# Block 0 of a convolution and GELU-MLP kernel in two column halves, with W_in in four parts, W_out right behind it, and the early x loads moved to the hardware DMA ring

## The chip, the cores and the metric

One core of a Trainium2 chip. The metric is device time of one execution in microseconds (us); smaller is better. Single executions of the kernel before agree within about 0.3% (685.96 to 687.88 us in the rounds of the experiments). The experiments ran on four chips; the kernel before ran in each round, and each time is held against it.

Names used below: PE is TensorE (matmul), PEld its weight load, DVE is VectorE, ACT ScalarE, POOL GpSimd, SP SyncE. DMA transfers issued by GpSimd go through the software ring (its queue moved 2.56 MB in the profile before, which is the sum of what GpSimd issued), those issued by SyncE and ScalarE through hardware rings (their queues moved 48.78 and 0.59 MB, again the sums of what each issued). A *block* is a stretch of tokens, 256 wide for blocks 0 to 5 and 512 wide after that, taken twice: once in each half of the tokens. A *third* is one of three groups of channels of a block's convolution. A *slice* is one of the pieces of the first multiply of a block, each ended by one GELU of 1024 columns.

## The reference

```python
def _attn_ref(x, weight):                  # x (8, 4096, 192), weight (8, 7)
    w = np.exp(weight - np.max(weight, axis=-1, keepdims=True))
    w = w / (np.sum(w, axis=-1, keepdims=True) + 1e-09)
    # causal convolution over the sequence, 7 taps, one set of taps per head of 24 channels
    ...
    out = np.einsum('hk,bskhg->bshg', w, x_unf)

def _moe_ref(x, w_in, w_out):              # x (32768, 192), w_in (192, 2048), w_out (2048, 192)
    h = x @ w_in
    g = 0.5 * h * (1.0 + erf(h * inv_sqrt2))
    return (g @ w_out).astype(np.float32)
```

Convolution, first multiply, exact GELU, second multiply. All tensors are float32; the kernel multiplies in bf16.

## The kernel before

For blocks 0 and 1 the convolution runs on PE, as multiplies with diagonal weights, 7 taps for each third and each of two row halves. From block 2 on it runs on VectorE, as a chain of fused multiply-adds. So VectorE must keep ahead of PE from then on, while it also takes the finished convolution of block 1 out of PSUM. The orders, cut out and put side by side:

```python
WS = [256] * 6 + [512] * ((HALF - 1536) // 512)
PC = {0: 0, 1: 1}                       # blocks convolved on PE
SW = {1: (2, 3), 2: (0, 2, 1, 3), 3: (0, 2, 1, 3)}   # x loads in the software ring
CONVB = {0: [0, 1, 2], 1: [3, 0, 1]}    # PSUM banks of the thirds
FP = [0, FQ, 2 * FQ, FH]                # W_in in three parts: 1/4, 1/4, 1/2 of a half

# GpSimd: order of its loads
for i in range(3):
    win_in(FP[i], FP[i + 1], S_WIN[i])
...
halo(0)
load(g, 1, SW[1], S_XG[1])
load(g, 2, SW[2], S_XG[2])
g.dma_start(<W_out>).then_inc(S_WOUT, 16)
halo(1)
load(g, 3, SW[3], S_XG[3])

# VectorE: order at the head
diag(0); diag(1)                        # diagonal weights
for p in range(NP): trans(0, p)         # 32x32 transposes of x
diag(2)
dup(0); dup(1); dup(2)                  # second copy of W_in for the other row half
for p in range(NP): trans(1, p)
for p in range(NP): cast(1, p)
# from here the list of block 2: transposes (op 0 to 2), then the convolution;
# evictions of block 1's thirds stand ahead of op 0, 3 and 5
side = [((2, (0, 3, 5)[p]), conv_out, 1, p) for p in range(NP)]

# PE: first multiply of block 0, with thirds of block 1 behind slices 4, 5, 6
for p in range(NP):
    behind[0, 4 + p] = [(1, p, k) for k in range(KS - 1, -1, -1)]

# SyncE
load(sp, 0, (0, 1))
sp.wait_ge(S_WIN[0], 32)
load(sp, 1, (0, 1))
sp.wait_ge(S_XG[3], 64)
for n in range(1, NB):
    if n + 3 < NB:
        load(sp, n + 3)
    ...
```

The order on VectorE: the eviction of block 1's first third, then three transposes of block 2's x, then the other two evictions.

## Time and profile before

| | before |
|---|---|
| time, median of 3 (range) | 686.16 us (686.04 to 686.56) |
| span of the profiled execution | 684.5 us |
| PE busy | 677.3 us (99%) |
| x of block 2 | software ring, ahead of W_out; VectorE doesn't wait for it |
| W_out | 768 KB, issue to landing 8.6 us |
| first second-multiply of block 0's values (taken together with block 1's first multiplies) | 21.11 us |

The last row is the *marker* of this document. From there PE is busy almost without a gap (55.43 of 55.50 us in the stretch that the prediction shows), so a shift of the marker should be a shift of the end. The times of landings and waits are of the profiled execution.

### The profile page before, as it was taken

How to read it: one execution, taken by the hardware profiler on the slowest of the kernel's cores; microseconds unless marked ns; L12 is line 12 of the kernel's file. 1: busy time of each engine (PE TensorE's matmuls, PEld its weight loads, DVE VectorE, ACT ScalarE, POOL GpSimd, SP SyncE). 2: the span in 40 equal slices, each digit the busy share in tenths (PEclk: the TensorE clock that was granted, in tenths of full speed). 3: DMA queues.
4: the chain of work that ended last, by engine and by line, in shares of the span. 5: the costliest groups of instructions: out<-in, count | busy, mean ns of one | idle time of the engine just before them, and what ended most of it. 6: DMA issues, size and time to landing. Idle time of an engine off the chain costs nothing.

```text
span 684.5 us, 27314 instructions
## 1 busy us (share of the span) xinstructions
PE 677.3 (99%) x12548; PEld 409.0 (60%) x12548; DVE 580.5 (85%) x914; ACT 532.6 (78%) x536; POOL 46.0 (7%) x97
## 2 busy tenths in 40 slices
PE   8999999999999999999999999999999999999997
PEld 4899655555555555555555555555555555555556
DVE  7999999888899888898888898888898888998702
ACT  6788987877787777787877878777778777877771
POOL 8110000000000000000000000000000000000000
PEclk9999999999999999999999999999999999999999
DMA  8544531344432344422444422444322444221224
GB/s 135 95 107 99 117 61 32 64 94 95 94 67 50 76 94 95 93 52 55 85 94 95 88 51 53 95 94 95 72 54 66 95 94 95 61 53 31 48 49 94
DMA packets 133234, 53.66 MB, mean 78 GB/s; under 512 B 127552, under 2 KB 132960, under 8 KB 133120
## 3 DMA queue, kind: packets, MB, share of 16 engines
q1 hardware_dynamic: 128144, 48.78, 33.3%
q0 software_dynamic: 3792, 2.56, 2.4%
q8 instruction: 98, 1.61, 1.0%
q10 hardware_dynamic: 1184, 0.59, 0.3%
q14 instruction: 16, 0.13, 0.1%
HBM read 28.31 MB, written 25.17 MB: 78 GB/s over the span
## 4 chain that ended last, share of the span: by engine, by line
PE 96%; ACT 2%; DMA 1%; issue 0%; DVE 0%; SPq 0%
PE hp L683 47%; PE ob L747 42%; PE ob L714 6%; ACT gT L612 2%; PE ob L640 1%; DMA xin<-in_x_dram 1%; ACT osb L227 0%; DVE osb L247 0%; SPq L258 0%; DVE osb L229 0%; DVE xT L478 0%; ACT xTb L572 0%; SPq L795 0%; ACT xc L579 0%
## 5 line engine op out<-in xcount | busy, mean ns | idle before, releaser
L612 ACT ACTIVATE gT<-hp 128x1024 bf16<-128x1024 f32 x512 | 523.4, 1024 | 132.7 <-PE hp L683 129.6
L683 PE MATMUL hp<-xc,win 64*64 64x512 bf16 (+2 forms) x6048 | 418.5, 366 | 1.1 <-ACT gT L612 0.7
L747 PE MATMUL ob<-gT,wout 64*64 64x512 bf16 x5376 | 366.3, 376 | 0.0
L508 DVE SCALAR_TENSOR_TENSOR acc<-xT,wcol,acc 128x512 f32<-128x512 f32 (+1 forms) x495 | 314.0, 697 | 0.0
L683 PEld LDWEIGHTS hp<-xc,win 64*64 64x64 bf16 (+1 forms) x6048 | 187.7, 106 | 135.6 <-ACT gT L612 2.1
L747 PEld LDWEIGHTS ob<-gT,wout 64*64 64x64 bf16 x5376 | 172.1, 118 | 123.0
L247 DVE STREAM_TRANSPOSE osb<-ob 128x512 f32<-128x512 f32 x84 | 73.7, 880 | 86.8 <-PE ob L747 86.8
L478 DVE STREAM_TRANSPOSE xT<-xin 128x512 f32<-128x512 f32 (+1 forms) x105 | 78.5, 799 | 0.2 <-DMA xin<-in_x_dram 0.2
L508 DVE SCALAR_TENSOR_TENSOR xc<-xT,wcol,acc 128x512 bf16<-128x512 f32 (+1 forms) x99 | 65.1, 711 | 0.0
L374 POOL COPY xT<-xT 128x558 f32<-128x558 f32 x33 | 21.6, 654 | 578.6 <-DVE xT L478 578.6
L501 DVE TENSOR_SCALAR acc<-xT,wcol 128x512 f32<-128x512 f32 (+1 forms) x99 | 56.1, 618 | 1.1
L714 PE MATMUL ob<-wout,gT 64*128 64x192 bf16 x1024 | 52.2, 243 | 0.3
L714 PEld LDWEIGHTS ob<-wout,gT 64*128 64x128 bf16 x1024 | 43.5, 94 | 6.5 <-PE ob L714 0.6
L357 POOL COPY xT<-xT 128x18 f32<-128x18 f32 x30 | 11.6, 387 | 1.4 <-DVE xc L461 1.4
L229 DVE COPY osb<-ob 128x384 f32<-128x384 f32 x4 | 2.2, 557 | 7.8 <-PE ob L714 7.8
L625 PE MATMUL hp<-warm 128*128 128x512 bf16 x16 | 5.7, 533 | 1.3 <-DVE warm L394 1.3
L640 PE MATMUL ob<-xTb,dg 64*64 64x256 bf16 x84 | 5.3, 271 | 1.1 <-ACT xTb L572 1.1
L227 ACT ACTIVATE osb<-ob 128x384 f32<-128x384 f32 x12 | 5.8, 486 | 0.0
L258 POOL DMA_DIRECT2D xin<-in_x_dram x10 | 5.8, 588 | 0.0
L640 PEld LDWEIGHTS ob<-xTb,dg 64*64 64x64 bf16 x84 | 4.3, 106 | 2.2 <-ACT xTb L572 1.6
L625 PEld LDWEIGHTS hp<-warm 128*128 128x128 bf16 x16 | 2.0, 129 | 4.5 <-issue 2.7
L324 POOL DMA_DIRECT2D win<-in_moe_w_in_dram x6 | 3.9, 651 | 0.0
(32 smaller groups left out, 21.7 us busy)
## 6 DMA issues: line engine op xcount, KB each, us to landing
xin<-in_x_dram SPq DMA_DIRECT2D x116, 192.0 KB, 4.4
out_dram<-osb SPq DMA_DIRECT2D x112, 192.0 KB, 3.6
out_dram<-osb SPq DMA_DIRECT2D x56, 48.0 KB, 1.7
xin<-in_x_dram SPq DMA_DIRECT2D x12, 96.0 KB, 2.7
xin<-in_x_dram POOLq DMA_DIRECT2D x10, 96.0 KB, 2.7
wout<-in_moe_w_out_dram POOLq DMA_DIRECT2D x1, 768.0 KB, 8.6
win<-in_moe_w_in_dram POOLq DMA_DIRECT2D x4, 96.0 KB, 4.2
win<-in_moe_w_in_dram POOLq DMA_DIRECT2D x2, 192.0 KB, 5.3
```

Source lines behind the costliest of these rows:

```text
L247: v.transpose(ap(osb[m % 2], j, [[8 * C, 128], [C // 2, TB // 32], [NP, 32]]), bank(ring(m, j)),).then_inc(S_EV)
L357: g.tensor_copy(dst, ap(xT[(n - 1) % 2], WS[n - 1] + 31, [[NP * XW, 128], [XW, NP], [32, HB]],),).then_inc(S_HALO)
L374: g.tensor_copy(ap(t, 1, [[NP * tw, 128], [tw, NP], [32, HB], [1, 31]]), ap(t, WS[n], [[NP * tw, 128], [tw, NP], [32, HB], [1, 31]]),).the ...
L478: v.transpose(ap(xT[n % 2], p * XW + HL, [[NP * XW, 128], [1, w]]), ap(xin[n % NX], p, [[TB // 32 * DQ, 128], [DQ, w // 32], [NP, 32]],),) ...
L501: ins = v.tensor_scalar(a, src, wk, None, ALU.mult)
L508: ins = v.scalar_tensor_tensor(dst, src, wk, a, op0=ALU.mult, op1=ALU.add)
L612: a.activation(out=ap(gT[n % 2], i * c * 2 * w, dst), in_=ap(hp[u % 2], 0, src), func=AF.Gelu,).then_inc(S_GELU)
L625: t.matmul(hp[1][:, 0:512], warm[:, 0:128], warm[:, :])
L640: ins = t.matmul(bank(CONVB[n][p], r, w), dg[r, d0 : d0 + 64], xTb[PC[n]][r, x0 : x0 + w], start=(k == KS - 1), stop=(k == 0), tile_positi ...
L683: ins = t.matmul(hp[u % 2][fo : fo + fw, o : o + w], win[r, f1 : f1 + fw], xc[n % 2][r, p * TB : p * TB + w], start=(p == 0), stop=(p == N ...
L714: ins = t.matmul(bank(bb[sub], w=C), gT[m % 2][r, c0 : c0 + 128], wout[r, CH[i] * C : (CH[i] + 1) * C], start=(ph == 0 and i == 0), stop=( ...
L747: ins = t.matmul(bank(ring(m, j), slice(64 * h, 64 * h + 64), w), ap(wout, 64 * hf * NF * C + CH[i] * C + j, [[NF * C, 64], [NP, 64]],), g ...
```

## The change

Its intent: block 0 is split into two halves of 128 columns, so that PE can begin the first multiply after half the convolution. W_in comes in four equal parts, so that slices wait for less. W_out follows it at once in the software ring. The x of blocks 1, 2 and 3 moves to SyncE's hardware ring, behind waits for W_in's fourth part (block 2) and for W_out (block 3); half of block 1's was there before. The x of block 0 is loaded as long rows, and ScalarE makes a third of the diagonal weights. Cut to its core:

```diff
+    PARTS = [(0, 0, 128, (0, 1, 2)), (0, 128, 128, (3, 0, 1)), (1, 0, 256, (2, 3, 0))]
-        SW = {1: (2, 3), 2: (0, 2, 1, 3), 3: (0, 2, 1, 3)}
-        FP = [0, FQ, 2 * FQ, FH]
+        FP = [0, FQ, 2 * FQ, 3 * FQ, FH]
 ... # load(): block 0 as one long row for each partition
+                if n == 0:
+                    dst = [[TB // 32 * DQ, 32], [1, mb * D - DQ]]
+                    src = [[mb * D, 32], [1, mb * D - DQ]]
 ... # GpSimd; the loop ahead of it still loads parts 0 to 2
             halo(0)
-            load(g, 1, SW[1], S_XG[1])
-            load(g, 2, SW[2], S_XG[2])
+            win_in(FP[3], FP[4], S_WIN[3])
             g.dma_start(<W_out>)
             halo(1)
-            load(g, 3, SW[3], S_XG[3])
 ... # VectorE
             diag(0)
+            trans(0, 0)
             diag(1)
-            for p in range(NP):
-                trans(0, p)
-            diag(2)
+            trans(0, 1)
+            trans(0, 2)
             dup(0)
             dup(1)
+            for p in range(NP):
+                cast(1, p)
             dup(2)
+            conv_out(1, 0)
+            dup(3)
+            conv_out(1, 1)
+            conv_out(1, 2)
             for p in range(NP):
                 trans(1, p)
             for p in range(NP):
-                cast(1, p)
+                cast(2, p)
 ... # ScalarE: third set of diagonal weights, casts and evictions of the first half
+            for k in range(KS):
+                a.activation(<64 columns of dg>, func=AF.Copy, scale=<one tap>)
+            cast0(0)
+            cast0(1)
+            conv_out0(0)
+            cast0(2)
+            conv_out0(1)
+            conv_out0(2)
 ... # PE: slices 0 to 3 are the first half, 4 to 7 the second, each 24 matmuls of 128 columns
-                behind[0, 4 + p] = [(1, p, k) for k in range(KS - 1, -1, -1)]
+            behind = {
+                1: third(1, 0),
+                2: third(1, 1) + third(1, 2),
+                4: third(2, 0),
+                5: third(2, 1),
+                6: third(2, 2),
+            }
 ... # SyncE
             sp.wait_ge(S_WIN[0], 32)
-            load(sp, 1, (0, 1))
-            sp.wait_ge(S_XG[3], 64)
+            load(sp, 1)
+            sp.wait_ge(S_WIN[3], 32)
+            load(sp, 2)
+            sp.wait_ge(S_WOUT, 16)
+            load(sp, 3)
```

More of the change, by code (lines that the diff above doesn't have):

```diff
@@ L128, in bass_lightweight_conv__then__act_gelu_exact_kernel @@
         ob = pst("ob", [128, 2048])
-        SW = {1: (2, 3), 2: (0, 2, 1, 3), 3: (0, 2, 1, 3)}
         S_WSB = sem("S_WSB")
-        S_WIN = [sem("S_WIN%d" % i) for i in range(3)]
+        S_WIN = [sem("S_WIN%d" % i) for i in range(4)]
         S_WOUT = sem("S_WOUT")
-        S_XG = {n: sem("S_XG%d" % n) for n in SW}
         S_XIN = [sem("S_XIN%d" % i) for i in range(NX)]
@@ L145, in bass_lightweight_conv__then__act_gelu_exact_kernel @@
         S_HOT = sem("S_HOT")
-        S_CAST = [sem("S_CAST%d" % i) for i in range(len(PC))]
+        S_CAST = [sem("S_CAST%d" % i) for i in range(len(PARTS))]
+        S_DGA = sem("S_DGA")
         S_PC = sem("S_PC")
@@ L163, in bank @@
             return ob[r, 512 * (b % 4) : 512 * (b % 4) + w]
-        CONVB = {0: [0, 1, 2], 1: [3, 0, 1]}
         NCV = NP * KS
@@ L170, in bass_lightweight_conv__then__act_gelu_exact_kernel, with pce @@
         FH = F // 2
-        FP = [0, FQ, 2 * FQ, FH]
+        FP = [0, FQ, 2 * FQ, 3 * FQ, FH]
         def cvd(n):
             return NCV * sum(m not in PC for m in range(n + 1))
-        def pce(n, p):
-            return NP * PC[n] + p + 1
+        def pce(i, p):
+            return NP * i + p + 1
         HC = [0]
@@ L190, in xin_at @@
         def xin_at(n):
-            return sum(64 - 16 * len(SW.get(m, ())) for m in range(n % NX, n + 1, NX))
+            return 64 * (n // NX + 1)
         def banks(m, g):
@@ L257, in load @@
                 off = ((q // 2) * HALF + OFF[n]) * D + DQ * (q % 2)
-                e.dma_start(
-                    ap(
-                        xin[n % NX],
-                        32 * q * (TB // 32 * DQ),
-                        [[TB // 32 * DQ, 32], [DQ, mb], [1, DQ]],
-                    ),
-                    ap(xt, off, [[mb * D, 32], [D, mb], [1, DQ]]),
+                dst = [[TB // 32 * DQ, 32], [DQ, mb], [1, DQ]]
+                src = [[mb * D, 32], [D, mb], [1, DQ]]
+                if n == 0:
+                    dst = [[TB // 32 * DQ, 32], [1, mb * D - DQ]]
+                    src = [[mb * D, 32], [1, mb * D - DQ]]
+                e.dma_start(
+                    ap(xin[n % NX], 32 * q * (TB // 32 * DQ), dst), ap(xt, off, src)
                 ).then_inc(sm or S_XIN[n % NX], 16)
@@ L349, in halo @@
                     if n - 2 in PC:
-                        g.wait_ge(S_PCE, pce(n - 2, NP - 1))
+                        g.wait_ge(S_PCE, pce(n - 1, NP - 1))
                     else:
@@ L450, in dup, with cast, conv_out @@
                     ).then_inc(S_DUPE)
-            def cast(n, p):
+            def cast(i, p):
+                n, c0, w, _ = PARTS[i]
                 v.wait_ge(S_TR, NP * n + p + 1)
                 v.tensor_copy(
-                    ap(xTb[PC[n]], p * XB + HL, [[NP * XB, 128], [1, WS[n]]]),
-                    ap(xT[n % 2], p * XW + HL, [[NP * XW, 128], [1, WS[n]]]),
-                ).then_inc(S_CAST[PC[n]])
-            def conv_out(n, p):
-                v.wait_ge(S_PC, pce(n, p))
+                    ap(xTb[PC[n]], p * XB + HL + c0, [[NP * XB, 128], [1, w]]),
+                    ap(xT[n % 2], p * XW + HL + c0, [[NP * XW, 128], [1, w]]),
+                ).then_inc(S_CAST[i])
+            def conv_out(i, p):
+                n, c0, w, bk = PARTS[i]
+                v.wait_ge(S_PC, pce(i, p))
                 v.tensor_copy(
-                    xc[n % 2][:, p * TB : p * TB + WS[n]], bank(CONVB[n][p], w=WS[n])
+                    xc[n % 2][:, p * TB + c0 : p * TB + c0 + w], bank(bk[p], w=w)
                 ).then_inc(S_PCE)
@@ L469, in trans @@
                         v.wait_ge(S_XIN[n % NX], xin_at(n))
-                    if n in SW:
-                        v.wait_ge(S_XG[n], 16 * len(SW[n]))
                     if n >= 2 and n - 2 in PC:
-                        v.wait_ge(S_PCE, pce(n - 2, NP - 1))
+                        v.wait_ge(S_PCE, pce(n - 1, NP - 1))
                     elif n >= 2:
@@ L482, in trans @@
                         p,
-                        [[TB // 32 * DQ, 128], [DQ, w // 32], [NP, 32]],
+                        [[TB // 32 * DQ, 128], [D if n == 0 else DQ, w // 32], [NP, 32]],
                     ),
@@ L533, in _ @@
             for p in range(NP):
-                cast(1, p)
-            side = [((2, (0, 3, 5)[p]), conv_out, 1, p) for p in range(NP)]
+                cast(2, p)
+            side = [((2, (0, 3, 5)[p]), conv_out, 2, p) for p in range(NP)]
             for n in range(M0, M1):
@@ L569, in _, with cast0, conv_out0 @@
             a.activation(out=hot[:, 1:2], in_=warm[0:1, 0:1], func=AF.Gelu).then_inc(S_HOT)
-            for p in range(NP):
+            a.wait_ge(S_PRO, 10)
+            a.wait_ge(S_IDN, 2)
+            for k in range(KS):
+                d0 = ((NP - 1) * KS + k) * 64
+                c0 = (NP - 1) * 32 + k
+                a.activation(
+                    out=dg[:, d0 : d0 + 64],
+                    in_=idb[:, :],
+                    func=AF.Copy,
+                    scale=wcol[:, c0 : c0 + 1],
+                ).then_inc(S_DGA)
+            _, _, w0, bk0 = PARTS[0]
+            def cast0(p):
                 a.wait_ge(S_TR, p + 1)
                 a.activation(
-                    out=ap(xTb[0], p * XB + HL, [[NP * XB, 128], [1, WS[0]]]),
-                    in_=ap(xT[0], p * XW + HL, [[NP * XW, 128], [1, WS[0]]]),
+                    out=ap(xTb[0], p * XB + HL, [[NP * XB, 128], [1, w0]]),
+                    in_=ap(xT[0], p * XW + HL, [[NP * XW, 128], [1, w0]]),
                     func=AF.Copy,
                 ).then_inc(S_CAST[0])
-            for p in range(NP):
+            def conv_out0(p):
                 a.wait_ge(S_PC, p + 1)
                 a.activation(
-                    out=xc[0][:, p * TB : p * TB + WS[0]],
-                    in_=bank(CONVB[0][p], w=WS[0]),
-                    func=AF.Copy,
+                    out=xc[0][:, p * TB : p * TB + w0], in_=bank(bk0[p], w=w0), func=AF.Copy
                 ).then_inc(S_PCE)
+            cast0(0)
[4 more added lines that the diff above has]
+            conv_out0(2)
             due = {(1, 6): [(0, 0)]}
@@ L599, in _ @@
                         a.wait_ge(S_MM2, MMC[n - 1])
-                    if M0 <= n < M1:
+                    g0 = i * c * 2 * w
+                    if n == 0:
+                        src = [[2 * TB, 128], [TB, 2], [128, 4], [1, 128]]
+                        dst = [[NF * 2 * TB, 128], [128, 2], [512, 4], [1, 128]]
+                        g0 = i % 4 * 4 * 512 + i // 4 * 256
+                    elif M0 <= n < M1:
                         src = [[2 * TB, 128], [1, 2 * TB]]
@@ L612, in _ @@
                     a.activation(
-                        out=ap(gT[n % 2], i * c * 2 * w, dst),
+                        out=ap(gT[n % 2], g0, dst),
                         in_=ap(hp[u % 2], 0, src),
@@ L625, in _, with pconv @@
                 t.matmul(hp[1][:, 0:512], warm[:, 0:128], warm[:, :])
-            def pconv(n, p, k):
-                w = WS[n]
+            def pconv(i, p, k):
+                n, c0, w, bk = PARTS[i]
                 if k == KS - 1:
-                    t.wait_ge(S_CAST[PC[n]], p + 1)
-                    if n == 0:
-                        t.wait_ge(S_DG, p + 1)
-                if k == KS - 2:
+                    t.wait_ge(S_CAST[i], p + 1)
+                    if i == 0:
+                        if p < NP - 1:
+                            t.wait_ge(S_DG, p + 1)
+                        else:
+                            t.wait_ge(S_DGA, KS)
+                if k == KS - 2 and c0 == 0:
                     t.wait_ge(S_HALO, HC[n] + 2 + p)
@@ L638, in pconv @@
                     d0 = (p * KS + k) * 64
-                    x0 = p * XB + 32 * k
+                    x0 = p * XB + 32 * k + c0
                     ins = t.matmul(
-                        bank(CONVB[n][p], r, w),
+                        bank(bk[p], r, w),
                         dg[r, d0 : d0 + 64],
@@ L649, in pconv, with third @@
                     ins.then_inc(S_PC)
-            taps = [(p, k) for p in range(NP) for k in range(KS - 1, -1, -1)]
-            for p, k in taps:
-                pconv(0, p, k)
-            behind = {}
+            def third(i, p):
+                return [(i, p, k) for k in range(KS - 1, -1, -1)]
             for p in range(NP):
-                behind[0, 4 + p] = [(1, p, k) for k in range(KS - 1, -1, -1)]
+                for q in third(0, p):
+                    pconv(*q)
+            behind = {
[5 more added lines that the diff above has]
+            }
             def mm1(n, i):
@@ L663, in mm1 @@
                     t.wait_ge(S_GELU, u - 1)
-                if i == 0:
-                    if n in PC:
-                        t.wait_ge(S_PCE, pce(n, NP - 2))
-                    else:
-                        t.wait_ge(S_CV, cvd(n))
-                if n == 0 and i in (0, 2, 4):
-                    t.wait_ge(S_WIN[i // 2], 32)
-                    t.wait_ge(S_DUPE, 2 * (i // 2) + 2)
+                part = {(0, 0): 0, (0, 4): 1, (1, 0): 2}.get((n, i))
+                if part is not None:
+                    t.wait_ge(S_PCE, pce(part, NP - 2))
+                elif i == 0:
+                    t.wait_ge(S_CV, cvd(n))
+                x0 = 0
+                if n == 0:
+                    w, c = 128, 4
+                    x0 = i // 4 * w
+                    if i < 4:
+                        t.wait_ge(S_WIN[i], 32)
+                        t.wait_ge(S_DUPE, 2 * i + 2)
                 for cc in range(c):
-                    f0 = 128 * CH[i * c + cc]
+                    f0 = 128 * CH[(i * c + cc) % NF]
                     for p in range(NP):
-                        if n in PC and i == 0 and cc == 0 and p == NP - 1:
-                            t.wait_ge(S_PCE, pce(n, p))
+                        if part is not None and cc == 0 and p == NP - 1:
+                            t.wait_ge(S_PCE, pce(part, p))
                         for hf in range(2):
@@ L685, in mm1 @@
                                     win[r, f1 : f1 + fw],
-                                    xc[n % 2][r, p * TB : p * TB + w],
+                                    xc[n % 2][r, p * TB + x0 : p * TB + x0 + w],
                                     start=(p == 0),
@@ L702, in mm2 @@
                         t.wait_ge(S_PH, PHC[m] + g + 1)
-                if g == 0 and ph == 0:
+                if m == 0:
+                    if ph == 0 and i == 0:
+                        t.wait_ge(S_GELU, 4 * g + 4)
+                elif g == 0 and ph == 0:
                     c = NCH[m]
@@ L775, in _ @@
                     mm1(n, i)
-                    for q in behind.get((n, i), []):
+                    for q in behind.get(i, []) if n == 0 else []:
                         pconv(*q)
```

## The prediction

> **What bounds the kernel now.** I read the page first: the matrix engine (PE) is busy 677.3 of 684.5 us and PE lines hold 96% of the chain that ended last. So only the start, the joins between stages and the end can give anything. Since the change edits the first two blocks only, I then read the chain of waits of the first 60 us.
>
> ```profile
> 2.04 4.96 DMA xin<-in_x_dram
> ...
> 7.03 0.53 DVE xT L478
> ...
> 7.58 0.43 ACT xTb L572
> ...
> 8.04 2.50 PE ob L640 x42
> ...
> 11.01 0.63 PE hp L683 x8
> ...
> 11.66 1.94 ACT gT L612 x2
> ...
> 13.61 1.03 ACT gT L612
> ...
> 14.69 0.83 PE hp L683 x12
> 15.51 0.88 PE ob L640 x14
> 16.40 0.76 PE hp L683 x12
> 17.16 0.88 PE ob L640 x14
> 18.04 0.76 PE hp L683 x12
> 18.80 0.88 PE ob L640 x14
> 19.68 1.42 PE hp L683 x24
> ```
>
> Columns: start, length, what. The head is serial to 11.0: x lands (7.0), transpose, cast, block 0's convolution on PE, eviction. Then three GELUs pace PE to 14.7. From 14.69 there is nothing but PE: four first multiplies and three thirds of block 1's convolution in turn, and the last entry is slice 7 of block 0 with slice 0 of block 1, so block 1 begins at about 20.35 (19.68 and half of 1.42, less the tail). All that this change can win lies before that moment; whatever it adds to PE after the first multiply is paid in full unless it fills PE's idle time.
>
> From the table of stretches: PE has no room after that.
>
> ```profile
> 24.50:80.00 55.50, 55.43 (x1134) 49.95 (x1132) 55.33 (x115) 46.79 (x54) 4.62 (x10) 1.00 0.46 100
> ```
>
> PE is busy 55.43 of 55.50 us, but VectorE (third pair, 55.33) is full too, so I looked in the timeline at where the two meet most closely, block 6, the first of width 512:
>
> ```profile
> 70.81 2.07 DVE L508 SCALAR_TENSOR_TENSOR xc<-xT,wcol,acc 128x512 bf16<-128x512 f32 x3
> ...
> 73.55 0.81 PE L683 MATMUL hp<-xc,win 64*128 64x512 bf16 x6
> ```
>
> VectorE ends block 6's convolution at 72.88, PE needs it at about 73.5: only 0.6 us of slack. A gain in PE's start reaches the end only if VectorE's run of convolutions moves with it.
>
> [...] twelve 256-wide matmuls (six pairs on two row halves) take 0.66 us, 110 ns a pair[...]; sixteen 192-wide ones 0.66, 82 a pair[...]. [...] In this trace loads of 64x128 last 92 to 96 ns and those of 64x64 102 to 107; the smaller is the slower[...]. The convolution's weights are 64x64. [...] x moves as 384-byte packets, 22 to 35 ns each in this trace's head, some 11 to 17 bytes per ns. [...] Trace: 256 elements in 384 to 417 ns, 1024 in 1024[...].
>
> **Part by part.**
>
> *Load of x, block 0.* Rows of 5760 B in place of 15 pieces of 384 B, twice the bytes (0.74 MB in all against 0.39). [...] I put the landing at 5.3 to 5.9, against 7.0. But VectorE's chain for the convolution weights ends at 5.64 and the first diagonal build (0.58) now comes first: transpose (0,0) runs 6.26 to 6.78, against 7.56 before, and (0,1), (0,2) end at 7.85 and 8.29, since the second build stands between. The last transpose before ended at 8.35: nothing gained there.
>
> *ScalarE.* Seven scaled copies of 64 columns replace VectorE's third build (0.58): about 0.3 us each, 0.25 apart, so 5.7 to 7.6. They hold back the first cast from 6.8 to 7.6. Casts and evictions of 128 are 107 ns shorter (0.31 and 0.28). In order: cast 0 to 7.9, cast 1 to 8.3, eviction 0 at 8.6 to 9.0, cast 2 to 9.3, eviction 1 to 9.6, eviction 2 at about 10.4. PE's third third waits for cast 2. The multiply's last operand is ready at 10.4 against 10.96: 0.55 us won.
>
> *Convolution, PE.* 42 matmuls more (84 of 128 wide and 42 of 256 instead of 84 of 256). At 256 wide a third takes 0.77 to 0.88. At 128 wide it is 7 pairs of 56 ns if the stream decides, 0.4; about 100 ns a pair if the 64x64 weight load does (107 seen, less a little overlap), 0.7. The new three thirds are thus 1.2 to 2.1 us more on PE.
>
> *First multiply, block 0.* Eight slices of 24 matmuls of 128 columns instead of 12 of 256. Stream-bound: 12 x 56 = 0.67 us a slice, as now. [...]
>
> *W_in and copies.* The last part is issued after block 0's halo, at about 8.75, and by the 2.4 to 4.2 us that loads in this ring take lands near 12.3. VectorE: copies of parts 0 and 1 (0.45 to 0.5 each half) to 10.1, casts of the second half to 10.8, part 2 to 11.8, then eviction (1,0), part 3, the other two evictions, three transposes (1.34), casts of block 1.
>
> *Weights out, early x.* W_out lands earlier (some 18 against 21.1), but the 0.29 us that the weight load waited for it leaves no gap on PE. x of blocks 2 and 3 comes later but before VectorE wants it. Nothing on the path.
>
> **The two sums.** *Stream-bound:* first multiply from 10.1; slice 2 ends at 12.6; slice 3 waits for part 3's copy (12.3 + 0.9), 13.2 to 13.9; slice 4 to 14.5; the convolution of block 1 waits for VectorE: 13.75, transposes to 15.1, cast to 15.5; then 3 x 0.77 + 3 x 0.68 = 4.4, block 1 begins at 19.9: 0.45 us earlier. [...] The difference passes whole to the end: VectorE's last eviction of block 1 follows the same third of the convolution, so its run of convolutions shifts with PE and the 0.6 us of slack stays.
>
> **Rivals.** *A gain by filling the idle PE:* between 8.04 and 14.69 PE does 5.1 us of work in 6.65, so 1.5 us is idle; with the head's 0.55 this would make 684.2 if nothing were added. [...] *x lands late:* twice the bytes against W_in in the same 16 engines, which are full from 5 us; if it lands at 7.5, everything moves 0.7 to 1.2 us later: about 688.5. For: the DMA share is near its top there. Against: fifteen times fewer pieces. *VectorE or part 3 of W_in becomes the bound:* part 3 late by 1 us adds up to 1 us in the stream-bound case[...]. *Hidden anyway:* block 6 waits for VectorE, and a gain over 0.6 us is lost there; caps the good case near 685.5.
>
> **Range and chances.** I give the two sums even weight: -0.45 and +2.15, mean +0.9 on 686.16: 687.1. The lower end takes the stream-bound sum with 0.5 us more luck, the upper the load-bound one with 0.6 us of bad luck. 2% is 13.7 us, more than the whole head but for a few us, so within 2% is all but sure.
>
> **What would show it.** [...] Thirds of the convolution at 128: 0.4 or 0.7. The transpose at 6.26 behind the diagonal build, not behind the load. First multiply's wait for the eviction over at 10.4. Start of block 1: 19.9 or 22.5, and every later block shifted by the same. I'm wrong if block 1 starts before 19.3, if a later block's wait eats or adds a shift, or if the time after the head changes.

The forecast of 687.1 us is the mean of two sums for the start of block 1. The stream-bound sum came to 19.9 us, 0.45 earlier than before. The load-bound sum came to about 22.5 us, 2.15 later. The trace before has no matmul 128 columns wide. The 56 ns a pair is what the changed kernel then showed (24 more matmuls took 0.67 us). The 100 ns a pair is an estimate from the 107 ns of the 64x64 weight loads. On ScalarE of the changed kernel the seven scaled copies took 333 ns each, 0.24 us apart, and casts and evictions of 128 columns 302 and 277 ns, against 417 and 384 for 256 columns before.

## More of the kernel before

VectorE's timeline before, around the x of block 2. The columns are start, length, engine, line, operation, output and inputs, count, and in brackets the idle time ahead of it with what ended it.

```profile
16.44 0.42 DVE L461 CAST xc<-ob 128x256 bf16<-128x256 f32 x1 [1.61 <-PE ob L640]
16.78 1.33 DVE L478 STREAM_TRANSPOSE xT<-xin 128x256 f32<-128x256 f32 x3
18.08 0.42 DVE L461 CAST xc<-ob 128x256 bf16<-128x256 f32 x1
```

The first line is the eviction of block 1's first third, the second the transposes of block 2, the third the second eviction. There is no bracket at the transposes: x was there.

## The result, and the profile after

| | before | after |
|---|---|---|
| time, median (range), 4 runs each, same chip | 686.36 us (686.04 to 686.72) | 689.88 us (689.59 to 690.09) |
| ratio after / before, 95% interval | | 1.0051 (1.0033 to 1.0068) |
| span of the profiled execution | 684.5 us | 688.2 us |
| marker | 21.11 us | 24.40 us |
| start of VectorE's last eviction | 681.08 us | 684.35 us |

Ratios are the mean time of one kernel's fast runs over that of the other's fast runs of the same rounds, so they are not quite the ratio of the medians quoted here. The change makes the kernel 3.5 us slower: within 2%, but outside the predicted range of 685.2 to 688.9.

The last two rows say where: the marker is 3.29 us later and the last eviction 3.27 us. Of the span's 3.8 us (688.23 against 684.45), all but some 0.5 us arises before the marker; that rest comes after the last eviction. The table of stretches of the changed kernel, moved by the same 3.3 us, confirms that nothing is lost between:

```profile
27.80:83.30 55.50, 55.43 (x1134) 49.91 (x1130) 55.32 (x115) 46.77 (x54) 4.61 (x10) 1.00 0.44 94
```

PE is busy 55.43 of 55.50 us, to the digit what it was before. So most of the question is the head. PE's timeline of the changed kernel there:

```profile
12.14 0.85 PE L725 MATMUL hp<-xc,win 64*128 64x128 bf16 x24 [0.67 <-DVE win L435]
12.91 0.97 PE L670 MATMUL ob<-xTb,dg 64*64 64x128 bf16 x28
14.76 1.52 PE L725 MATMUL hp<-xc,win 64*128 64x128 bf16 x48 [0.87 <-DVE win L435]
...
20.81 0.84 PE L725 MATMUL hp<-xc,win 64*128 64x128 bf16 x24
22.90 0.40 PE L725 MATMUL hp<-xc,win 64*128 64x256 bf16 x4 [1.25 <-DVE xc L459]
23.95 0.61 PE L725 MATMUL hp<-xc,win 64*128 64x256 bf16 x8 [0.66 <-DVE xc L459]
24.40 0.66 PE L759 MATMUL ob<-wout,gT 64*128 64x192 bf16 x12
```

Three things are to be seen. Slices 2 and 3 wait 0.67 and 0.87 us for VectorE's copies of W_in (for the first of these waits, see r5). The groups of 24 and 48 matmuls give the cost of a 128-wide matmul: 24 more take 1.52 - 0.85 = 0.67 us, which is 56 ns for each pair on the two row halves. And between block 0 and block 1 there are two new waits, 1.25 and 0.66 us, for VectorE's evictions of block 1's convolution. VectorE's timeline tells why these were late:

```profile
17.60 0.43 DVE L459 CAST xc<-ob 128x256 bf16<-128x256 f32 x1 [0.46 <-PE ob L670]
21.11 1.34 DVE L474 STREAM_TRANSPOSE xT<-xin 128x256 f32<-128x256 f32 x3 [3.08 <-DMA xin<-in_x_dram]
22.34 0.41 DVE L459 CAST xc<-ob 128x256 bf16<-128x256 f32 x1
...
23.49 0.41 DVE L459 CAST xc<-ob 128x256 bf16<-128x256 f32 x1
```

VectorE is free at 17.60 + 0.43 = 18.03 and then waits 3.08 us for the x of block 2, although the thirds that it has to evict are finished at about 19.2 and 20.9 (the ends of their groups on PE). The transposes stand ahead of them in its order. The chain of waits leads back from there:

```profile
8.55 0.58 POOL win L322
9.12 4.59 DMA win<-in_moe_w_in_dram
...
13.73 0.56 SPq L261
...
15.64 5.45 DMA xin<-in_x_dram
...
21.11 1.34 DVE xT L474 x3
```

W_in's fourth part is issued at 8.55, behind block 0's halo, and lands at 13.7. Only then may SyncE issue the x of block 2, and the last of that lands at 21.1. In the DMA view of 14 to 17 us, the columns being packets, MB, and share of 16 engines' time, the software ring with W_out has nearly everything:

```profile
q0 software_dynamic: 1334, 0.51, 148.9%
q1 hardware_dynamic: 11, 0.00, 1.1%
```

So there are two suspects in one: x of block 2 is issued late, and it is issued behind W_out. Before, neither held. The ring also changed the form of the load: by the packet lists of the traces, x of block 2 is 1024 packets of 384 bytes in the hardware ring, and 64 of 4224 and 64 of 1920 bytes in the software ring. Besides these: the waits for W_in in block 0, the matmuls of half width, and the 0.5 us at the end.

### The profile page after: what moved, and what is told of

It reads as the page before. It is cut to its first block, busy times and chain, and to the rows that moved or that the text cites. A ratio compares the mean times of both kernels' runs of the same rounds, so it can differ in the third digit from the quotient of the medians.

```text
span 688.2 us, 27608 instructions
## 1 busy us (share of the span) xinstructions
PE 678.6 (99%) x12686; PEld 410.8 (60%) x12686; DVE 581.6 (84%) x921; ACT 533.2 (77%) x543; POOL 41.5 (6%) x89
## 4 chain that ended last, share of the span: by engine, by line
PE 94%; DMA 2%; ACT 1%; DVE 1%; issue 0%; SPq 0%; POOL 0%
PE hp L725 47%; PE ob L792 42%; PE ob L759 5%; DMA xin<-in_x_dram 1%; ACT gT L639 1%; DMA win<-in_moe_w_in_dram 1%; DVE xT L474 0%; SPq L261 0%; ACT osb L224 0%; ACT L560 0%; DVE osb L244 0%; DVE xc L459 0%; DVE acc L497 0%; POOL win L322 0%; DVE osb L226 0%
## 5 line engine op out<-in xcount | busy, mean ns | idle before, releaser
L725 PE MATMUL hp<-xc,win 64*64 64x512 bf16 (+3 forms) x6144 | 418.9, 363 | 3.7 <-DVE xc L459 1.9
L670 PE MATMUL ob<-xTb,dg 64*64 64x128 bf16 (+1 forms) x126 | 6.2, 238 | 0.4 <-DVE xTb L451 0.3
L435 DVE COPY win<-win 64x768 bf16<-64x768 bf16 x8 | 3.5, 438 | 1.8 <-DMA win<-in_moe_w_in_dram 1.6
```

Of the source, the lines that this page charges most:

```text
L670: ins = t.matmul(bank(bk[p], r, w), dg[r, d0 : d0 + 64], xTb[PC[n]][r, x0 : x0 + w], start=(k == KS - 1), stop=(k == 0), tile_position=(64 ...
L725: ins = t.matmul(hp[u % 2][fo : fo + fw, o : o + w], win[r, f1 : f1 + fw], xc[n % 2][r, p * TB + x0 : p * TB + x0 + w], start=(p == 0), st ...
```

## The experiments

The *theory*: the loss is the order of the loads (x of block 2 late), and the halves cost some tenths of a us. The *rivals*: the halves cost most of it; or W_in's fourth part does. The marker separates the head from the tail; where two runs are compared by it, the text says so.

### 1. e1_x2_early: the x of block 2 issued right behind that of block 1

```diff
             load(sp, 1)
-            sp.wait_ge(S_WIN[3], 32)
             load(sp, 2)
```

> The changed kernel with one wait taken out: SyncE issues block 2's load of x right behind block 1's, instead of behind the landing of W_in's last part (13.7 us). Theory A (most of the loss is VectorE's 3.1 us wait for block 2's x, which is stuck behind W_out in the DMA engines; it holds back the evictions of block 1's convolution): x of block 2 lands by 16, VectorE's wait at 21.1 goes, block 1's second multiply starts at 22.0 to 22.4 instead of 24.4, total 687.4 to 687.9 (2.0 to 2.4 less than the changed kernel). Rival B (the loss is the 42 added convolution matmuls and the halved slices on PE): PE stays where it is, at most 0.6 us less. Rival C (late W_in): block 0's waits grow by x's traffic, total 689 or more.

Measured: 688.45 us against 686.03, ratio 1.0036 (1.0019 to 1.0053); marker 22.55. The gain on the changed kernel is there, 1.85 us by the marker, but smaller than expected, because x still comes too late. VectorE's timeline and the DMA view of 14 to 17 us of this kernel:

```profile
19.27 1.33 DVE L474 STREAM_TRANSPOSE xT<-xin 128x256 f32<-128x256 f32 x3 [1.53 <-DMA xin<-in_x_dram]
```

```profile
q0 software_dynamic: 1054, 0.40, 112.5%
q1 hardware_dynamic: 382, 0.14, 26.2%
```

Early issue alone doesn't bring it in time: the four loads are issued from 9.77 on, and W_out's packets still outnumber theirs. Over these 3 us the hardware ring had 382 of 1436 packets here, and 11 of 1345 in the changed kernel. The trace doesn't show when the packets of x were ready in their ring, so how the engines shared themselves out between the two rings is not shown.

### 2. e2_win3_early: W_in's fourth part with the other three

```diff
-            for i in range(3):
+            for i in range(4):
                 win_in(FP[i], FP[i + 1], S_WIN[i])
 ...
             halo(0)
-            win_in(FP[3], FP[4], S_WIN[3])
 ...
-            sp.wait_ge(S_WIN[3], 32)
+            sp.wait_ge(S_PCE, pce(1, NP - 1))
             load(sp, 2)
```

The x of block 2 was tied to the second half's evictions, so that it would not come earlier as well.

> The changed kernel with W_in's fourth part issued with the other three, ahead of block 0's halo; block 2's x stays late (it waits for block 1-half evictions, about 14 us, so it is issued as late as before). Theory A: PE's two waits for VectorE's copies in block 0 (0.67 and 0.87 us) shrink by about 0.9 us in all, but VectorE still waits for block 2's x until 20 to 21, and the gain is swallowed there: total within 0.9 us below the changed kernel, only as far as W_out and so x come earlier. Rival C (late W_in part is what costs): PE's block 0 ends 0.8 us earlier and the total falls by 0.8 to 1.5, with VectorE's wait for x gone.

Measured: 690.40 against 686.03, ratio 1.0066 (1.0051 to 1.0081); marker 24.54, no better than the change: a miss. PE's waits for W_in are gone, but a stop took their place which the next run has too. In both runs it holds PE past the landing of x, so that VectorE no longer waits for x, and neither tests the theory.

### 3. e3_both: both edits, x early and W_in's fourth part early

The wait ahead of `load(sp, 2)` goes as in e1, the fourth part moves as in e2.

> Both edits: block 2's x early and W_in's fourth part early. Theory A with the W_in wait as its second term: block 1's second multiply at 21.0 to 21.6 (21.1 in the kernel before), total 686.2 to 686.8, no longer clear of the kernel before. If the halves themselves cost PE time (rival B), it stays over 688.

Measured: 690.16 against 686.03, ratio 1.0057 (1.0042 to 1.0072); marker 24.99. A miss. PE's timeline, and its table of stretches (busy time of PE, PEld, DVE, ACT and POOL, then granted clock, DMA share, GB/s):

```profile
13.60 1.51 PE L724 MATMUL hp<-xc,win 64*128 64x128 bf16 x47
17.75 0.21 PE L724 MATMUL hp<-xc,win 64*128 64x128 bf16 x1 [2.64 <-issue]
```

```profile
15.00:18.00 3.00, 0.36 (x7) 0.11 (x4) 1.12 (x4) 0.51 (x1) 1.07 (x3) 1.00 1.19 180
18.00:21.50 3.50, 3.50 (x48) 2.75 (x48) 1.66 (x4) 1.89 (x2) 0.54 (x1) 0.55 0.20 45
```

PE stops for 2.64 us (2.09 in e2) one matmul ahead of a slice's end, waiting for nothing that the profile shows, and then runs at a granted clock of 0.55. In this trace one packet of 16 KB of kind *instruction* moves from 15.45 to 16.41 (15.01 to 15.96 in e2), and PE goes on 1.34 us after its end in both; in the changed kernel that packet moves at 13.06, in no one's way. In e2 and e3 W_out's packets begin at 11.0, a microsecond earlier than in the changed kernel (12.1), because W_in's fourth part no longer stands between block 0's halo and W_out. That PE waited for this packet, and that the packet was held behind W_out's, is the author's reading of the times of packets; no run took the packet alone away, and what it carries isn't shown. W_out's packets beside it are not enough: in e4, r7, r8, t1 and t4 a 16 KB instruction packet moves at 15.4 to 17.9, amid them, and PE doesn't stop. (The packet times in the expectation of r6 below, 11.3, 12.4 and 13.4, are 0.3 us too late on the scale of the other views.)

### 4. e4_whole: e3, and block 0 whole again

```diff
-    PARTS = [(0, 0, 128, (0, 1, 2)), (0, 128, 128, (3, 0, 1)), (1, 0, 256, (2, 3, 0))]
+    PARTS = [(0, 0, 256, (0, 1, 2)), (1, 0, 256, (3, 0, 1))]
 ... # GELU layout, waits and slices of block 0 as in the kernel before
-                1: third(1, 0),
-                2: third(1, 1) + third(1, 2),
-                4: third(2, 0),
-                5: third(2, 1),
-                6: third(2, 2),
+                4: third(1, 0),
+                5: third(1, 1),
+                6: third(1, 2),
```

> As the run with both edits, but block 0 is convolved and multiplied whole (256 columns) again: all load changes, x rows and the diagonals on ScalarE stay. My reckoning: first multiply at about 10.0 us, slices 0 to 3 paced by GELU, no added convolution; VectorE free of three casts and three evictions has block 1's transposes done at 13.2 and casts from 13.6; block 1 starts at about 18.5 to 19 and its second multiply at 19.2 to 19.8; total 684.3 to 685.0, faster than both. If the halves were the useful part of the change, it is slower than the run with both edits.

Measured: 688.04 against 686.03, ratio 1.0028 (1.0013 to 1.0043); marker 23.34. A miss: x of block 2 lands at 20.06 and VectorE waits 3.09 us for it, x of block 1 holds it 1.69 us. So a whole block 0 with these loads is no cure, and the loads have to be settled first.

### 5. r5_x2_ahead: the changed kernel with x of block 2 in the software ring ahead of W_out

```diff
+        S_XG2 = sem("S_XG2")
 ... # GpSimd
             win_in(FP[3], FP[4], S_WIN[3])
+            load(g, 2, (0, 2, 1, 3), S_XG2)
             g.dma_start(<W_out>)
 ... # SyncE
             load(sp, 1)
-            sp.wait_ge(S_WIN[3], 32)
-            load(sp, 2)
 ... # VectorE: waits for S_XG2 at block 2, the counts of that buffer's semaphore adjusted
```

> The changed kernel with one thing put back: block 2's x goes through the software ring ahead of W_out, as before the change. Theory A: x of block 2 lands by 16, VectorE does not wait for it (3.1 us in the changed kernel), W_out lands later (about 21.5); block 1's second multiply at 22.0 to 22.5 instead of 24.4, total 687.5 to 688.2. If it stays above 689, the late x was not the cause, only a symptom beside a busy PE.

Measured: 687.53 against 686.22, ratio 1.0013 (0.9998 to 1.0028); marker 21.73. The time is as expected, the marker a little earlier (22.0 to 22.5), and the interval no longer tells the run from the kernel before. VectorE's wait is gone, and the marker is 2.67 us earlier than in the changed kernel:

```profile
17.53 1.33 DVE L478 STREAM_TRANSPOSE xT<-xin 128x256 f32<-128x256 f32 x3
```

```profile
21.73 0.66 PE L763 MATMUL ob<-wout,gT 64*128 64x192 bf16 x12
```

Of the 2.67 us, 1.91 are the two waits ahead of block 1. Some 0.4 came with W_in's fourth part: VectorE's copy of it starts at 12.89 in place of 13.74, and the pair of slices behind it at 14.32 in place of 14.76. GpSimd issues W_out at 12.28 here and at 9.74 in the changed kernel, so W_out's early start probably slowed that part; no run shows that alone. The remaining 0.3 is the same 36 matmuls in one piece: 1.50 us here, 0.84 + 0.40 + 0.61 in three pieces there.

Slice 2 doesn't wait here at all. In the changed kernel VectorE's casts of the second half, which stand ahead of the copy for slice 2, meet GpSimd's issue of W_out; two of them last 871 and 801 ns, and here none over 253. The casts in the changed kernel, GpSimd's issue there, and the casts in r5:

```profile
10.00 1.08 DVE L451 CAST xTb<-xT 128x128 bf16<-128x128 f32 x3
```

```profile
9.74 1.25 POOL L380 DMA_DIRECT2D wout<-in_moe_w_out_dram  x1
```

```profile
10.17 0.50 DVE L453 CAST xTb<-xT 128x128 bf16<-128x128 f32 x3
```

### 6. r6_x2_ahead_win3: r5, and W_in's fourth part with the others

> As the run above, with W_in's fourth part issued with the other three. In the two runs that had W_in's last part early, PE stopped for 2.1 and 2.6 us at 15.2 us for nothing that the profile names, one 16 KB packet of the instruction queue came 2 us later than in the changed kernel, W_out's packets having begun at 11.3 instead of 12.4, and the granted clock then fell to a half for 3.4 us. Theory D: the instruction fetch stands behind W_out's packets. Here W_out begins at about 13, so the fetch at 13.4 is ahead of it: no stop, second multiply of block 1 at 21.0 to 21.6, total 686.2 to 687.0. If the stop comes from the changed order of PE's own work, it appears here too, total 689 to 690.

Measured: 687.53 against 686.22, ratio 1.0013 (0.9996 to 1.0030); marker 21.68, the same as r5. There is no stop: the instruction packet begins at 12.72 and W_out's packets at 12.79. The hoped-for gain didn't come; a copy of W_in slowed down in its place. VectorE's timeline; the view of the line of these copies (count, then shortest, median and longest in ns); then PE's timeline:

```profile
10.56 1.75 DVE L436 COPY win<-win 64x768 bf16<-64x768 bf16 x2
```

```profile
L436 DVE COPY win<-win x8: 419/422/1181, 8.1 to 13.0; 64x768 bf16<-64x768 bf16 x8
```

```profile
12.46 0.85 PE L728 MATMUL hp<-xc,win 64*128 64x128 bf16 x24 [0.82 <-ACT gT L642]
```

Two copies took 1.75 us, against 0.88 in the changed kernel: one of them, which takes 420 ns elsewhere, lasted 1181, and it lies beside GpSimd's issue of W_out (10.87 to 12.07). It recurs: in every run here in which a copy begins during that issue, one of them lasts until 0.22 to 0.25 us after the issue's end (834 ns in r5, 956 or 957 in e2, e3 and e4, 1175 in r8, some 1182 in r7, t2 and t4). Where none does, the longest of this size is 543 (t1) to 565 (t3), and 562 in the changed kernel, where the casts above were hit instead. What slows them isn't shown, and not everything that begins during the issue is slow: of the three casts in the changed kernel the first took 227 ns. PE waits 0.82 us ahead of slice 2. The bracket names the second GELU, which came last by the profile, but the slice needs only the first of the two, over at about 11.5; the copy ends at 10.56 + 1.75 = 12.31, just before the slice.

### 7. r7_whole_x2_ahead: r6, and block 0 whole

> As the last, but block 0 whole. The halves cost PE a third convolution part (about 1.3 us) and put the casts of block 1 behind 1.1 us of casts and 0.7 us of evictions on VectorE. I expect block 1's second multiply at 20.3 to 20.8, total 685.3 to 686.0: at or just below the kernel before, 0.5 to 1 us under the run with halves. If the halves were what pays, it is 0.5 us or more slower than that run.

Measured: 685.98 against 686.22, ratio 0.9990 (0.9975 to 1.0005); marker 20.84.

```profile
20.84 0.66 PE L745 MATMUL ob<-wout,gT 64*128 64x192 bf16 x12
```

r6 and r7 ran in the same rounds and differ in the halves alone. So the halves cost 21.68 - 20.84 = 0.84 us at the marker and 1.55 us of time. Of the rest some 0.5 lies at the end of the kernel, see below. The 0.84 isn't the matmuls' alone: r6 has the 0.82 us wait for the slow copy in it. Between t2 and t4 below, halves and whole each with its casts rearranged, the marker differs by 0.52.

### 8. r8_before_x2_late: the kernel before, with only the x of block 2 moved

```diff
-        SW = {1: (2, 3), 2: (0, 2, 1, 3), 3: (0, 2, 1, 3)}
+        SW = {1: (2, 3), 3: (0, 2, 1, 3)}
-            load(g, 2, SW[2], S_XG[2])
 ... # SyncE
             load(sp, 1, (0, 1))
+            sp.wait_ge(S_WIN[2], 32)
+            load(sp, 2)
```

> The reverse: the kernel before with block 2's x taken out of the software ring (it stood ahead of W_out) and put on SyncE behind W_in's landing, as the change does; nothing else. Theory A: W_out now runs from about 12.5 to 19, x of block 2 trickles behind it to 18 to 20 instead of 14.2, VectorE waits 1.5 to 3 us for it at 16.8, block 1's evictions follow late; total 687.0 to 688.5, 1 to 2.3 us over the kernel before. If it is within 0.4 us of the kernel before, the late x costs nothing by itself.

Measured: 689.18 against 686.22, ratio 1.0041 (1.0022 to 1.0059); marker 23.50. VectorE's timeline:

```profile
20.22 1.32 DVE L477 STREAM_TRANSPOSE xT<-xin 128x256 f32<-128x256 f32 x3 [3.48 <-DMA xin<-in_x_dram]
```

One load moved in the old kernel, with no halves in it, costs 2.8 us by the ratio (its interval is 1.5 to 4.0 us), of the change's 3.5, and moves the marker by 2.39. It is issued from 10.31 on, against 10.19 in the kernel before, and lands at 20.20 against 14.35: the late issue has no part in this, only the place beside W_out and the other ring. This and r5 settle the main cause from both sides; the ring's small packets and W_out's place change together in both. The cost was above the upper expectation of 688.5.

### 9. t1_whole_tuned: r7 with another order

ScalarE casts all thirds before it evicts; VectorE transposes and casts block 1 ahead of W_in's fourth copy; the thirds of block 1 stand behind slices 2, 3 and 4.

```diff
-                4: third(1, 0),
-                5: third(1, 1),
-                6: third(1, 2),
+                2: third(1, 0),
+                3: third(1, 1),
+                4: third(1, 2),
```

> From the best run so far (block 0 whole, all W_in early, block 2's x ahead of W_out in the software ring): ScalarE casts all three parts before its first eviction, VectorE does block 1's transposes and casts ahead of W_in's last copy (needed only by slice 6), and block 1's convolution thirds stand behind slices 2, 3, 4 instead of 4, 5, 6, where PE idles for GELU. By that run's trace: 0.2 to 0.3 us from the third third's wait for its cast, 0.6 us of PE idle between 13.3 and 14.6 filled; block 1's second multiply at 19.9 to 20.2 instead of 20.84, total 685.0 to 685.4, some 0.8 to 1.2 under the kernel before. If block 1's x or the copies are late, nothing is won and it stays at 685.8 to 686.2.

Measured: 687.65 against 686.32, ratio 1.0016 (1.0003 to 1.0028); marker 22.11. A miss. x of block 1 lands at 12.84, so PE waits for its cast, and then the GELUs pace the last slices, which now have nothing between them. PE's timeline:

```profile
14.40 0.95 PE L663 MATMUL ob<-xTb,dg 64*64 64x256 bf16 x14 [1.25 <-DVE xTb L452]
...
20.53 1.75 PE L714 MATMUL hp<-xc,win 64*128 64x256 bf16 x24 [0.47 <-ACT gT L632]
```

### 10. t2_halves_tuned: r6 with fewer casts

ScalarE casts 256 columns at once and all thirds before it evicts, which frees VectorE of the second half's casts, and VectorE transposes block 1 between the evictions of the second half.

```diff
-            for p in range(NP):
-                cast(1, p)
             dup(2)
-            conv_out(1, 0)
             dup(3)
-            conv_out(1, 1)
-            conv_out(1, 2)
+            conv_out(1, 0)
             for p in range(NP):
                 trans(1, p)
+            conv_out(1, 1)
+            conv_out(1, 2)
```

> The same idea with the halves kept: ScalarE casts block 0 256 wide (VectorE's three casts of the second half go), VectorE does all W_in copies first and block 1's transposes ahead of the second half's last two evictions. Slice 2 no longer waits for its copy (0.8 us) and block 1's casts come 1.2 us sooner: second multiply at 19.6 to 20.3 instead of 21.7, total 685.2 to 686.0 (all kernels with halves have ended 0.4 us later behind their last matmul). If the halves cannot be made to pay because the third convolution part is real PE work, it lies at or above the tuned whole version.

Measured: 686.77 against 686.32, ratio 1.0004 (0.9990 to 1.0017); marker 21.10, as in the kernel before. PE waits 0.98 us ahead of slice 4 for an eviction of the second half. A miss (685.2 to 686.0 expected). The best of the versions with halves; it doesn't beat the kernel before.

### 11. t3_wout_waits: the changed kernel with W_out held until x of block 2 is there

```diff
             win_in(FP[3], FP[4], S_WIN[3])
+            g.wait_ge(S_XIN[2], 64)
             g.dma_start(<W_out>)
```

> The changed kernel with W_out's issue held until block 2's x has landed; that load is still issued at 13.7 us on SyncE as in the changed kernel. If W_out's packets are what held x back, x now lands 3 to 4 us after its first issue, at 17.0 to 17.8 (21.1 in the changed kernel), VectorE does not wait, and block 1 then waits for W_out instead (landing at 25 to 26): second multiply at 25 to 26, total 690 to 691. If x was late because it was issued late or went through the hardware ring, it lands at 20 or later here too.

Measured: 693.81 against 686.32, ratio 1.0106 (1.0088 to 1.0125), in one timed round. The time says nothing about the theory: GpSimd's wait also held back the halo of block 1, which stands behind it in GpSimd's order, and PE waited 4.54 us for that. What the run does show is the landing of x without W_out, in the chain of waits and in the DMA view of 14 to 17 us:

```profile
15.04 3.78 DMA xin<-in_x_dram
```

```profile
q1 hardware_dynamic: 1023, 0.37, 51.1%
```

The four loads are issued from 13.13 on, 0.6 us earlier than in the changed kernel, and the last lands at 18.82, between the two outcomes that were expected (17.0 to 17.8, or 20 and later). So of the 21.1 of the changed kernel, W_out is worth some 1.7 us (21.1 - 18.8 - 0.6). That W_out alone is enough to make x late is shown by e1 (19.27) and r8. That the late issue alone is enough isn't: of the 64 arrivals that VectorE waits for, 63 are in by 17.70, before the 18.03 at which the changed kernel wants x, and one straggler in a single profiled execution makes the 18.82.

### 12. t4_whole_casts_first: r7, ScalarE casting all thirds before the first eviction

```diff
             cast0(0)
             cast0(1)
-            conv_out0(0)
             cast0(2)
+            conv_out0(0)
             conv_out0(1)
```

> The best run (block 0 whole, all W_in early, block 2's x ahead of W_out) with one edit: ScalarE casts the third part of block 0 before its first eviction. The run that moved three things at once had its first multiply's last operand at 10.60 instead of 10.91 from this, and lost that and more where it put block 1's convolution in front of the slices that GELU paces. Alone I expect 0.3 us: second multiply of block 1 at 20.5 to 20.6, total 685.5 to 685.9, below the kernel before by 0.4 to 0.7 us. If it stays at 20.84, PE's chain behind slice 4 hangs on something other than the first multiply.

Measured: 685.73 (685.71 to 685.91) against 686.25, ratio 0.9986 (0.9973 to 1.0000); marker 20.58. This is the fastest version: block 0 whole, all of W_in first, x of block 2 ahead of W_out again, long rows of x, part of the diagonal weights on ScalarE. Its median is half a us under the kernel before's, as expected, but the interval's end touches 1.

## Why the prediction was wrong

**The step that failed:** "x of blocks 2 and 3 comes later but before VectorE wants it. Nothing on the path." VectorE wants x of block 2 at 18.03 and has it at 21.11, and the two evictions behind it then cost PE the waits of 1.25 and 0.66 us. I gave no time for its landing. The numbers were at hand: W_in's fourth part at 12.3 by the prediction itself; then four issues of some 0.6 us, so the last at about 14.1; then 2.7 us for a load (the old page's median), or 5.6 for the loads that the old kernel issued behind W_out. That is 16.8 to 19.7, against 16.78 at which VectorE began these transposes before. And the two evictions behind the transposes would have put it on PE's path. r8 shows this cost alone, 2.39 us at the marker; r5 takes it away again, 2.67.

**What the 3.29 us at the marker consist of.** The runs form a ladder from the changed kernel to the one before, each step one edit, but for the last, which is all the rest. The last column is the time over the kernel before, from the ratios:

| step | marker us | difference | time over before, us |
|---|---|---|---|
| changed kernel | 24.40 | | 3.5 |
| r5: x of block 2 ahead of W_out | 21.73 | 2.67 | 0.9 |
| r6: W_in's fourth part early | 21.68 | 0.05 | 0.9 |
| r7: block 0 whole | 20.84 | 0.84 | -0.7 |
| before: the rest of the edits undone | 21.11 | -0.27 | 0 |

At the marker the order of the loads is about four fifths, the halves a quarter, and what is left of the change is a small gain. By the time the loads are 2.6 and the halves 1.6 of 3.5 us, since the end of the kernel is longer in most runs with halves. Each marker is of one profiled execution, and each time is uncertain by about 1 us, so the last step is within the noise.

**The two sums.** Both took the matmuls as the uncertain term. The shorter time, "if the stream decides", was right, whatever the reason: 56 ns a pair, 0.67 us a slice, and a third of 128 columns costs 0.97 - 0.58 = 0.39 us. The even weight for the load-bound sum was misplaced: its longer time for a matmul of 128 columns had not been shown, and did not happen. That the mean of +0.9 has the right sign is luck: it came from a cost that wasn't there. The stream-bound sum, with block 1 at 19.9, left out the wait that came to decide.

**The terms before that.** Right in time, but by luck: the transpose begins at 6.14 (6.26 predicted), behind the load and not behind the diagonal build, which ends at 5.91; x lands at 6.12, where the prediction's estimate was 5.3 to 5.9. The old load had 8 pieces in a row, not 15: ScalarE's queue has 448 packets fewer (96 against 544 from 2 to 9 us), 7 for each of its 64 rows. Better than predicted: the last operand of the first multiply is ready by 9.45 in place of 10.4, and the scaled copies on ScalarE run from 5.29 to 7.07 (5.7 to 7.6 predicted). Predicted too early: W_in's fourth part, 12.3 and measured 13.7, which shows as the wait of 0.87 us in slice 3; and W_out itself, "some 18", which lands at 19.8. The 0.67 us in slice 2 is another term that the prediction lacks: the casts that meet GpSimd's issue of W_out (r5). The rival "VectorE or part 3 of W_in becomes the bound" was therefore partly right; moved away alone (e2, r6) it gave nothing, because a stop (e2) or a slow copy (r6) took its place. The rival of idle PE time took 5.1 us of work between 8.04 and 14.69; the table of stretches has PE busy for 5.73 there, so 0.9 us was idle, not 1.5.

**After the head.** "The difference passes whole to the end" was right: 3.29 us at the marker, 3.27 at the last eviction. "The 0.6 us of slack stays" was not quite: in the changed kernel VectorE ends block 6's convolution 3.78 us later than before, PE reaches its first multiply 3.28 later, so that 0.17 us of slack is left.

```profile
74.59 2.07 DVE L504 SCALAR_TENSOR_TENSOR xc<-xT,wcol,acc 128x512 bf16<-128x512 f32 x3
```

```profile
76.83 0.81 PE L725 MATMUL hp<-xc,win 64*128 64x512 bf16 x6
```

**The chances** (within 2% "all but sure") were right. The range was too narrow, for a spread over one term only.

**What stays open.** The last 0.5 us: in the changed kernel and the runs with halves, but not in t2, the time from the start of the last eviction to the end is 3.85 to 4.13 us, against 3.37 to 3.45 in the others. By the packet lists, each of these runs, and none of the others, has an 8 KB instruction packet 1.9 us before its end (at 686.30 in the changed kernel), while the last stores are under way; in t2 it comes 1.7 us after the end. That the packet delays the stores is argued from this, and no run tested it. Nor is it shown that the stop of e2 and e3 is a wait for their instruction packet.

## What to carry to other kernels

When a load moves to another ring or behind another wait, work out its landing time from its new issue time and from what runs in the DMA engines meanwhile, and hold it against the moment at which its reader is free; then look at what stands behind the reader in the same engine's order, for that is what is delayed. A large weight load that nobody needs soon belongs behind the small loads that somebody does: here x of block 2 beside W_out, and in the other ring, cost 2.39 us at the marker in r8, and r5 took 2.67 away. Splitting a stage to start earlier has to win more than it adds in casts, evictions and waits; here it lost 0.84 us at the marker, part of it to a slow copy, and its best version did not beat the kernel before.
